# Earlier start-up work, layer norm ahead of low parts, and the first two groups' scores moved into the last projection units of an attention-plus-MLP kernel

## The chip, the cores and the metric

One core of a Trainium2 chip runs the whole layer in one launch. The metric is the time of the launch in microseconds (us), the median over runs. TensorE does matrix products and transposes (PE in the profile), VectorE elementwise work and reductions (DVE), ScalarE activations and copies (ACT), GpSimd the rest of the elementwise work (POOL); SyncE issues every DMA (SP).

## The reference

```
h  = x + softmax_attention(layernorm(x) @ wqkv) @ wo
h2 = h + silu(layernorm(h) @ w1) @ w2
```

`x` is 2048 rows by 512 in float32, `wqkv` 512 by 1536, `wo` 512 by 512, `w1` 512 by 1792 and `w2` 1792 by 512. There are 32 heads of 16 columns, the scores are scaled by 16 to the power of -0.5, and the softmax runs over all 2048 keys. The layer norm has no weights, and its epsilon is 1e-5.

## The kernel before

**Precision.** A float32 product with weights is made of three products: every operand is split into a high part and a low part (the rest), and high x high, low x high and high x low are summed in PSUM (`product`). The high part is a rounded copy; `low` subtracts it from the source on DVE. Queries and keys are split into two float16 parts, which lie beside each other in the 48 rows that the score products contract over (`sh` and `sl` in `project_qk`).

**Start.** Rows come in four blocks `b` of 512, each block in four tiles `t` of 128 rows. `load_x(0)`, then the weights of values, keys and queries (`raw_v`, `raw_qk`, 256 KB a DMA), then `load_x(1)` stand in that order in SP's queue. Block 0's layer norm is made of `statistics` (two DVE instructions and two small POOL instructions, which leave `mv` and `rs`) and `normalize` (one DVE instruction over 128x512). TensorE turns a normalized tile (four 128x128 transposes into `ps_tr`), ACT copies the high part (`xth`), DVE subtracts the low part (`xtl`). The values of block 0 are summed first over the high parts (16 products), then with the low parts (32 more). `square` and `measure` find one scale for queries and keys.

**Blocks.** For each block, two units project the first 128 columns of keys and of queries (`project_qk`, 12 products of 128x512 each), and for blocks 1 to 3 four units project the values (`project_v`). Behind a unit stand, in program order, `burst` (maxima, below), then the statistics, normalizations and turns of the next block's rows (`first_ln`, `other_ln`). In block 0 the low part of a query or key unit is on DVE; from block 1 on it is on POOL (1.17 us), in whose queue the small `rs` instructions of the next layer norm stand too. Queries and keys go to DRAM (`kd`, `qd`) and come back per head into `ks` and `qs`.

**Units.** Then come 24 units that project the rest of queries and keys (`for g in range(1, NG // 2)`).

**Maxima.** The softmax needs a bound for each row. A maximum is one score product of 128 queries by 512 keys (`ps_m`) and one DVE reduction (`mx`); there are 64 for each of the 32 items (an item is four heads and one block of queries). They are spread over the whole kernel: `BESIDE_V` says how many stand behind each unit of blocks 1 to 3, `BESIDE_A` how many stand after which product of the 24 units, and in the attention stage a planner (`maxima`) gives each group a number.

**Attention.** A group is one item and 128 keys: four score products (`ps_s`, 64 rows of the array each), four exponentials on ACT (`pt`), and, two groups later (`LAG`), four products with the values (`values`, into `pv`). The twelve `pt` tiles come from one pool. Groups 0 to 4 take four maxima each in the planner; the others take at most three. Between items 8, 16 and 24, and at the end, an MLP block runs.

**PSUM.** Eight banks are given out by pools that are opened anew for each stage: `st` (3) and `sm` (5) in the blocks, `st` (2) and `sm` (6) in the 24 units, `pv` (1), `sm` (3) and `st` (4) in the attention. A tile waits until whoever read its bank before is done. All engines run their instructions in the order in which the program issues them.

Of the kernel before, what the change touches and what calls it, by code (L numbers as in the profile page):

```python
# [20 lines left out]
P = 128  # L21
# [20 lines left out]
PTS = 12  # L42

RING = 5

# [13 lines left out]

BESIDE_V = (0, 4), (0, 4), (6, 5)  # L60

BESIDE_A = {6: 6}, {4: 4}

# [8 lines left out]
def attention_mlp_kernel(ctx: ExitStack, tc: tile.TileContext, x, wqkv, wo, w1, w2, out):  # L72
# [249 lines left out]


    with ExitStack() as pa:
# [39 lines left out]

        def measure():
# [5 lines left out]
            pool("tensor_tensor", qk_s, qk_s, expo, ALU.pow)  # L371
            dve("tensor_scalar", qk_s, qk_s, TOP / 23.0, None, op0=ALU.mult)
            dve("tensor_scalar", qk_s.bitcast(U32), qk_s.bitcast(U32), 0x7F800000, None, op0=ALU.bitwise_and)
            dve("reciprocal", qk_e, qk_s)
            dve("scalar_tensor_tensor", qk_e, qk_e, SCALE, qk_e, op0=ALU.mult, op1=ALU.mult)
            pin(nc.scalar.reg_load(qk_f, qk_e[:1, :].bitcast(U32)))

        def project_qk(b, n, beside={}, scale=False):

            g, key = divmod(n, 2)  # L380
            cols = slice(key * D + g * P, key * D + (g + 1) * P)
            ps = bank("ps_qk")
            weave(product(ps, lambda c: wqk_h[:, c, cols], lambda c: wqk_l[:, c, cols],
                          lambda c: xth[b][:, c, :], lambda c: xtl[b][:, c, :], DC),
                  {k: (lambda n=n: burst(n)) for k, n in beside.items()})
# [32 lines left out]

        found = [statistics(xts[0][:, t, :]) for t in range(4)]
        for t in range(4):  # L420
            normalize(xts[0][:, t, :], xts[0][:, t, :], *found[t])
            act("copy", wv_h[:, t, :], raw_v[:, t, :])

        def columns(t):
            return slice(t * P, (t + 1) * P)

        def turn_high(b, t):
# [11 lines left out]
        ps_vs = [bank("ps_v", "st" if t < 3 else "sm") for t in range(4)]  # L439
        for t in range(4):  # L440
            for c in range(DC):
                mm(ps_vs[t], xth[0][:, c, columns(t)], wv_h[:, c, :], start=c == 0, stop=False)
        for n in (1, 0):
            split_qk(n)
        for n in range(NG):
            square(n)
        found = {}
        for t in range(6):
            if t < 4:
                found[t] = statistics(xts[1][:, t, :])  # L450
            if 0 < t < 5:
                normalize(xts[1][:, t - 1, :], xts[1][:, t - 1, :], *found.pop(t - 1))
        for t in range(4):
            for c in range(DC):
                mm(ps_vs[t], xth[0][:, c, columns(t)], wv_l[:, c, :], start=False, stop=False)
                mm(ps_vs[t], xtl[0][:, c, columns(t)], wv_h[:, c, :], start=False, stop=c == DC - 1)
            act("copy", va[:, t, :, 0:DH], ps_vs[t].rearrange("p (h d) -> p h d", d=DH))
            if t > 0:
                ps = turn_high(1, t - 1)
                low(xtl[1][:, :, columns(t - 1)], ps, xth[1][:, :, columns(t - 1)])  # L460
            if t == 0:
                load_x(2)
        measure()

        splits = {(0, 0): 2, (0, 1): 4, (1, 1): 6, (1, 5): 3, (2, 4): 5, (2, 5): 7}

        first_ln = {0: ((), (), (3,)), 1: ((), (), ())}
        other_ln = {0: ((0, 1), (0,), ()), 1: ((2, 3), (1,), (0,)), 2: ((), (2,), (1,)), 3: ((), (3,), (2,)),
                    4: ((), (), (3,)), 5: ((), (), ())}
        for b in range(NB):  # L470
# [3 lines left out]
            for n, (kind, k) in enumerate(units + vs if b else units):  # L474
                tick()
                if kind == "v":
# [11 lines left out]
                if b + 1 < NB:  # L488
                    rows = xts[b + 1]
                    stats, norms, turns = (other_ln if b else first_ln)[n]  # L490
                    for t in stats:
                        found[t] = statistics(rows[:, t, :])
                    for t in norms:
                        normalize(rows[:, t, :], rows[:, t, :], *found.pop(t))
                    for t in turns:
                        turn_x(b + 1, t)
                if (b, n) in splits:
# [7 lines left out]

        pb.close()
        at["blocks"] = False
        open_banks(pa, 1, st=2, sm=6)
        for g in range(1, NG // 2):
            for m, (b, key) in enumerate([(b, 1) for b in range(NB)] + [(b, 0) for b in range(NB)]):  # L510
                tick()
                if g == 1 and m < 2:
                    fixed_rows(2 + m)

                n = 8 * g + m - 12
                project_qk(b, 2 * g + key, BESIDE_A[n == 19], True)
                if 0 <= n < 8:
# [6 lines left out]
    cpool = ctx.enter_context(tc.tile_pool(name="cpool", bufs=1, side="right"))  # L524
    bp = ctx.enter_context(tc.tile_pool(name="bp", bufs=PTS))
    gp = ctx.enter_context(tc.tile_pool(name="gp", bufs=2))
# [5 lines left out]
    htl = cpool.tile([P, DC, 512], F32R, name="htl")  # L532
    groups = ITEMS * KC
    pts, den = {}, {}

    def scores(g, k, kind="st"):

        i, c = divmod(g, KC)
        a, j = HEADS[k]
        assert i in placed  # L540
        ps = bank("ps_s", kind)
        mm(ps, ks[i % RING][64 * j:64 * j + 64, a, c * P:(c + 1) * P], qs[i % RING][64 * j:64 * j + 64, a, :],
           start=True, stop=True)
        pts[g, k] = bp.tile([P, 512], F32, name="pt")
        act("activation", pts[g, k], ps, AF.Exp, scale=qk_f)

    def values(g):
# [129 lines left out]
    def gate(ps, engine="dve"):  # L677
        g, gh, gl = (bp.tile([P, 512], dt, tag="pt", name=name)
                     for name, dt in (("g", F32), ("gh", F32R), ("gl", F32R)))
# [100 lines left out]
    def finish_last(pending):  # L780
# [4 lines left out]

        o_t = bp.tile([P, 4, P], F32, tag="pt", name="o_t")
        pool("memset", o_t[:, :, :64], 0.0)
# [109 lines left out]
    def maxima(g):  # L897
# [106 lines left out]
```

## Time and profile before

| what | value |
| --- | --- |
| median of 3 runs | 1692.24 us |
| lowest, highest | 1691.54 us, 1692.86 us |
| the profiled execution, its own time | 1694.05 us |
| its span, first to last instruction | 1692.3 us |
| its mean granted TensorE clock | 0.998 |
| PE, DVE, ACT, POOL busy | 98%, 86%, 73%, 16% |

The profiled execution's time is 1.75 us longer than its span: that much lies around the instructions. A row of the timeline has the start, the length, the engine, the line, the operation, the tiles as written <- read, how often it follows itself, and in brackets how long the engine had been idle and what ended that. Of a run of equal instructions the length reaches from the first start to the last end. A row of the windows has a stretch, its length, then for PE, PE's weight loads, DVE, ACT and POOL the busy time and the number of instructions, the granted clock, the share of the DMA engines that was busy, and GB/s.

### The profile page before, as it was taken

The numbers are of one execution on the slowest core, as the hardware profiler recorded it, in microseconds if no ns is written. First come the engines' busy times: TensorE is split into PE (matmuls) and PEld (weight loads), VectorE is DVE, ScalarE is ACT, GpSimd is POOL, SyncE is SP. The second block draws the span as 40 slices with busy tenths as digits, with TensorE's granted clock in tenths as the row PEclk, the third lists the DMA queues.
The fourth block names the chain that finished last, engine by engine and source line by source line (L and its number), as shares of the span: only waits on it lengthen the run. The fifth ranks groups of instructions, "written<-read, shape, count | busy, mean of one in ns | idle before, by whom it ended". The sixth has DMA issues, their size and how long they took to land.

```text
span 1692.3 us, 28327 instructions
## 1 busy us (share of the span) xinstructions
PE 1660.4 (98%) x10498; PEld 645.5 (38%) x10498; DVE 1455.0 (86%) x2428; ACT 1242.2 (73%) x2443; POOL 269.7 (16%) x441
## 2 busy tenths in 40 slices
PE   7999999999999999999999999999999999999999
PEld 6666422222245532222245532222245542222377
DVE  6899999999978889999978889999978889997343
ACT  5323599999963279999953369999963379999743
POOL 3123400000033310000033310000034310000000
PEclk9999999999999999999999999999999999999999
DMA  4434311121222111111222211111222211100222
GB/s 175 118 82 156 113 34 41 37 50 38 63 59 89 59 49 32 36 50 38 61 59 80 69 49 32 36 44 44 60 61 79 69 49 31 35 11 20 58 82 81
DMA packets 100618, 102.81 MB, mean 61 GB/s; under 512 B 19076, under 2 KB 77252, under 8 KB 100480
## 3 DMA queue, kind: packets, MB, share of 16 engines
q1 hardware_dynamic: 100480, 101.01, 20.4%
q8 instruction: 82, 1.34, 0.3%
q14 instruction: 56, 0.46, 0.1%
HBM read 77.72 MB, written 17.29 MB: 56 GB/s over the span
## 4 chain that ended last, share of the span: by engine, by line
PE 88%; ACT 7%; DVE 3%; DMA 1%; issue 1%; SPq 0%; POOL 0%; ACTq 0%; POOLq 0%
PE pv L79 34%; PE ps_s L79 19%; PE ps_m L79 11%; PE ps_acc L79 10%; ACT pt L93 6%; PE ps_qk L79 5%; PE ps_wo L79 3%; PE ps_v L79 3%; PE ps_w L79 2%; DVE mx L219 2%; PE ps_tr L82 1%; SPq L99 0%; DVE pvs L96 0%; DMA ks<-in_A_x_dram 0%; DMA ks<-kd 0%
## 5 line engine op out<-in xcount | busy, mean ns | idle before, releaser
L219 DVE TENSOR_REDUCE mx<-ps_m 128x1 f32<-128x512 f32 x2009 | 1257.4, 682 | 89.1 <-PE ps_m L79 63.1
L93 ACT ACTIVATE pt<-ps_s 128x512 f32<-128x512 f32 x2048 | 1012.8, 608 | 21.8 <-PE ps_m L79 14.9
L79 PE MATMUL ps_s<-qs,ks 64*128 64x512 f16 x2048 | 535.6, 379 | 5.5 <-ACT pt L93 2.4
L79 PE MATMUL pv<-pt,va 128*17 128x512 f32 x4096 | 538.2, 599 | 1.2
L79 PE MATMUL ps_m<-ks,qs 48*128 48x512 f16 x2009 | 506.7, 381 | 4.1 <-DVE mx L219 3.6
L79 PEld LDWEIGHTS <-ks 64*128 64x128 f16 x2048 | 148.8, 94 | 546.9 <-issue 437.6
L79 PEld LDWEIGHTS pv<-pt,va 128*17 128x17 f32 x4096 | 68.7, 95 | 227.4 <-issue 209.8
L79 PEld LDWEIGHTS <-qs 48*128 48x128 f16 x2048 | 118.4, 94 | 69.0 <-issue 64.2
L93 ACT CAST w2h<-w 128x512 fp32r<-128x512 f32 x56 | 34.8, 621 | 101.8 <-PE ps_acc L79 101.8
L93 ACT ACTIVATE g<-pv 128x512 f32<-128x512 f32 x39 | 23.3, 597 | 102.2 <-PE pv L79 102.2
L79 PE MATMUL ps_acc<-w2l,gh 128*128 128x512 f32 x224 | 92.8, 414 | 0.0
L79 PE MATMUL ps_acc<-w2h,gh 128*128 128x512 f32 x224 | 91.8, 410 | 0.0
L79 PE MATMUL ps_acc<-w2h,gl 128*128 128x512 f32 x224 | 88.0, 393 | 0.0
L86 POOL TENSOR_TENSOR w2l<-w,w2h 128x512 fp32r<-128x512 f32 x42 | 53.7, 1280 | 164.4 <-ACT w2h L93 164.4
L96 DVE TENSOR_TENSOR gl<-g,gh 128x512 fp32r<-128x512 f32 x53 | 37.0, 699 | 48.5 <-ACT gh L93 48.5
L93 ACT ACTIVATE ks<-ps_qk,qk_s 128x512 f32<-128x512 f32 x30 | 20.7, 689 | 71.7 <-PE ps_qk L79 68.8
L79 PE MATMUL pv<-htl,w1h 128*128 128x512 f32 x156 | 65.5, 420 | 0.0
L86 POOL TENSOR_SCALAR nm<-nm 128x16 f32<-128x16 f32 x51 | 12.9, 253 | 328.5 <-DVE nm L229 325.2
L86 POOL TENSOR_TENSOR mx<-mx 128x32 f32<-128x32 f32 x38 | 9.5, 250 | 345.2 <-DVE mx L219 343.6
L79 PE MATMUL pv<-hth,w1h 128*128 128x512 f32 x156 | 62.3, 399 | 0.0
L86 POOL TENSOR_TENSOR ot<-ot,den 128x512 f32<-128x512 f32 (+1 forms) x16 | 20.4, 1274 | 257.9 <-DMA den<-dr 227.1
L79 PE MATMUL pv<-hth,w1l 128*128 128x512 f32 x156 | 61.3, 393 | 0.0
(125 smaller groups left out, 1386.3 us busy)
## 6 DMA issues: line engine op xcount, KB each, us to landing
w<-in_B_w_dram SPq DMA_DIRECT2D x112, 256.0 KB
ks<-kd SPq DMA_DIRECT2D x120, 192.0 KB
qs<-qd SPq DMA_DIRECT2D x128, 48.0 KB
kd<-sh SPq DMA_DIRECT2D x16, 256.0 KB
qd<-sh SPq DMA_DIRECT2D x16, 256.0 KB
hx<-in_A_x_dram SPq DMA_DIRECT2D x16, 256.0 KB
out_dram<-ot SPq DMA_DIRECT2D x16, 256.0 KB
ot<-pvs SPq DMA_DIRECT2D x124, 32.0 KB
```

Of the source, the lines that this page charges most:

```text
L79: tc.keep_in_program_order(nc.tensor.matmul(*a, **k))
L82: tc.keep_in_program_order(nc.tensor.transpose(*a))
L86: tc.keep_in_program_order(getattr(nc.gpsimd, op)(*a, **k))
L93: pin(getattr(nc.scalar, fn)(*a, **k))
L96: pin(getattr(nc.vector, fn)(*a, **k))
L219: pin(nc.vector.tensor_reduce(mx[i][:, j, a, qt, kb:kb + 1], ps, axis=AX.X, op=ALU.max))
```

## The change

1. At the start, 24 and then 8 transposes of the identity are put ahead of and behind the first tile's transposes (`idle`). The first tile is normalized after two tiles' statistics instead of four; products with the high parts begin between the transposes; two of the four copies of the values' weights go from ACT to POOL. Squares are spread out; only two of block 1's tiles are turned ahead of `measure`, the other two behind the first key unit.
2. In units of queries and keys the next block's statistics and normalizations are issued ahead of the projection (`layer_norm`), and so ahead of its low part in POOL's queue. Turns stay behind the maxima.
3. `BESIDE_V` rises from (0, 4), (0, 4), (6, 5) to (0, 4), (2, 4), (6, 6): 72 maxima instead of 64. In the last block the first of each burst takes an `st` bank. In the first four of the 24 units, the six maxima stand after product 10, 9, 8 and 7 instead of 6.
4. The eight score products of groups 0 and 1 stand in the last two of the 24 units, each followed by a maximum: three after product 3 and three after product 9 of the last but one (with one maximum more), two after product 4 of the last (with four maxima more). They use `sm` banks. The planner gives groups 0 and 1 nothing, and the others at most three. By the end of group 4, 226 maxima are done in both kernels: 206 and 20 before, 217 and 9 after. From group 5 on, the numbers per group are the same.
5. `wv_h` and `wv_l` get a pool of their own on the right side of SBUF, and 8 of the 12 `pt` tiles take that place; the other 4 stay where `pt` was.

```diff
+EARLY = 8
-BESIDE_V = (0, 4), (0, 4), (6, 5)
-BESIDE_A = {6: 6}, {4: 4}
+BESIDE_V = (0, 4), (2, 4), (6, 6)
+BESIDE_A = {6: 6}
+BESIDE_A1 = 10, 9, 8, 7
...
+    def pt_tile(name, dtype=F32):
+        pool_of = pools[next(taken) % PTS >= EARLY]
+        return pool_of.tile([P, 512], dtype, tag="pt", name=name)
...
+        wvp = pb.enter_context(tc.tile_pool(name="wvp", bufs=1, side="right"))
-        wv_h = wp.tile([P, DC, D], F32R, name="wv_h")
-        wv_l = wp.tile([P, DC, D], F32R, name="wv_l")
+        wv_h = wvp.tile([P, DC, D], F32R, name="wv_h")
+        wv_l = wvp.tile([P, DC, D], F32R, name="wv_l")
...
+        def idle(n):
+            ps = bank("ps_i")
+            for c in range(n):
+                tr(ps[:, columns(c % 4)], ident, ident)
...
-        turned = [turn_high(0, t) for t in range(4)]
+        idle(24)
+        found = [statistics(xts[0][:, t, :]) for t in range(2)]
...
+        first_rows(0)
+        idle(8)
+        for c in range(2):
+            act("copy", wv_h[:, c, :], raw_v[:, c, :])
+        found += [statistics(xts[0][:, t, :]) for t in range(2, 4)]
+        for c in range(2, 4):
+            pool("tensor_copy", wv_h[:, c, :], raw_v[:, c, :])
+        first_rows(1)
+        first_products(0, 0)
+        first_rows(2)
+        first_products(0, 1)
+        first_rows(3)
...
-        measure()
+        turned = [turn_high(1, t) for t in range(2)]
+        measure(lambda: normalize(xts[1][:, 3, :], xts[1][:, 3, :], *found.pop(3)))
+        for t in range(2):
+            low(xtl[1][:, :, columns(t)], turned[t], xth[1][:, :, columns(t)])
...
-        first_ln = {0: ((), (), (3,)), 1: ((), (), ())}
+        first_ln = {0: ((), (), (2, 3)), 1: ((), (), ())}
...
                 else:
+                    layer_norm()
                     project_qk(b, k, scale=b > 0)
...
-                    burst(BESIDE_V[b - 1][kind == "v"])
+                    burst(BESIDE_V[b - 1][kind == "v"], *[bank("ps_m")] * (b == NB - 1))
+                if kind == "v":
+                    layer_norm()
+                for t in turns:
+                    turn_x(b + 1, t)
...
+        first_scores = [(g, m ^ (g % 2)) for g in range(LAG) for m in range(4)]
+        def begin_scores(n):
+            for _ in range(n):
+                g, k = first_scores.pop(0)
+                scores(g, k, "sm")
+                one_max(1 - HEADS[k][1])
+        BESIDE_T = {3: lambda: begin_scores(3), 9: lambda: (begin_scores(3), burst(1))}, {4: lambda: (begin_scores(2), burst(4))}
...
+        pools.append(ctx.enter_context(tc.tile_pool(name="bp0", bufs=EARLY, side="right")))
...
+                beside = {BESIDE_A1[m]: 6} if g == 1 and m < len(BESIDE_A1) else BESIDE_A
+                if n >= 18:
+                    beside = BESIDE_T[n - 18]
...
-        if g < LAG + 3:
-            at["due"] = 1
-            return 4
-        if g in marks or g - 1 in marks:
+        if g < LAG or g in marks or g - 1 in marks:
             return 0
```

More of the change, by code (lines that the diff above doesn't have):

```diff
@@ L321, in weave, with scores @@
                 inserts[k + 1]()
+    groups = ITEMS * KC
+    pts, den, pools = {}, {}, []
+    taken = iter(range(10 ** 6))
+    def pt_tile(name, dtype=F32):
+        pool_of = pools[next(taken) % PTS >= EARLY]
+        return pool_of.tile([P, 512], dtype, tag="pt", name=name)
+    def scores(g, k, kind="st"):
+        i, c = divmod(g, KC)
+        a, j = HEADS[k]
+        assert i in placed
+        ps = bank("ps_s", kind)
+        mm(ps, ks[i % RING][64 * j:64 * j + 64, a, c * P:(c + 1) * P], qs[i % RING][64 * j:64 * j + 64, a, :],
+           start=True, stop=True)
+        pts[g, k] = pt_tile("pt")
+        act("activation", pts[g, k], ps, AF.Exp, scale=qk_f)
     with ExitStack() as pa:
@@ L384, in project_qk @@
                           lambda c: xth[b][:, c, :], lambda c: xtl[b][:, c, :], DC),
-                  {k: (lambda n=n: burst(n)) for k, n in beside.items()})
+                  {k: n if callable(n) else (lambda n=n: burst(n)) for k, n in beside.items()})
             sh = xp.tile([P, 512], F16, name="sh")
@@ L417, in attention_mlp_kernel @@
         load_x(1, parts=4)
[L419 to L422, printed above, removed]
         def columns(t):
             return slice(t * P, (t + 1) * P)
+        def idle(n):
+            ps = bank("ps_i")
+            for c in range(n):
+                tr(ps[:, columns(c % 4)], ident, ident)
         def turn_high(b, t):
@@ L432, in turn_high, with first_rows, first_products @@
             return ps
-        turned = [turn_high(0, t) for t in range(4)]
+        idle(24)
+        found = [statistics(xts[0][:, t, :]) for t in range(2)]
+        turned, ps_vs = [], []
+        def first_rows(t):
+            normalize(xts[0][:, t, :], xts[0][:, t, :], *found[t])
+            turned.append(turn_high(0, t))
+        def first_products(t, *chunks):
+            if t == len(ps_vs):
+                ps_vs.append(bank("ps_v", "st" if t < 3 else "sm"))
+            for c in chunks:
+                mm(ps_vs[t], xth[0][:, c, columns(t)], wv_h[:, c, :], start=c == 0, stop=False)
+        first_rows(0)
[10 more added lines that the diff above has]
+        first_rows(3)
+        for chunks in ((0, 1), (2,), (3,)):
+            for t in range(2):
+                if t or chunks != (0, 1):
+                    first_products(t, *chunks)
+        for t in range(2, 4):
+            first_products(t, *range(DC))
         for c in range(DC):
@@ L438, in attention_mlp_kernel @@
             low(xtl[0][:, :, columns(t)], turned[t], xth[0][:, :, columns(t)])
-        ps_vs = [bank("ps_v", "st" if t < 3 else "sm") for t in range(4)]
-        for t in range(4):
[L441 to L451, printed above, removed]
+        keys = [n for n in range(NG) if n % 2]
+        split_qk(1)
+        for n in keys[:3]:
+            square(n)
+        split_qk(0)
+        found = {}
+        for t in range(4):
+            found[t] = statistics(xts[1][:, t, :])
+            if t:
                 normalize(xts[1][:, t - 1, :], xts[1][:, t - 1, :], *found.pop(t - 1))
@@ L457, in attention_mlp_kernel @@
             act("copy", va[:, t, :, 0:DH], ps_vs[t].rearrange("p (h d) -> p h d", d=DH))
-            if t > 0:
-                ps = turn_high(1, t - 1)
-                low(xtl[1][:, :, columns(t - 1)], ps, xth[1][:, :, columns(t - 1)])
             if t == 0:
                 load_x(2)
-        measure()
+                for n in (*keys[3:], *range(0, NG, 2)):
+                    square(n)
+        turned = [turn_high(1, t) for t in range(2)]
+        measure(lambda: normalize(xts[1][:, 3, :], xts[1][:, 3, :], *found.pop(3)))
+        for t in range(2):
+            low(xtl[1][:, :, columns(t)], turned[t], xth[1][:, :, columns(t)])
         splits = {(0, 0): 2, (0, 1): 4, (1, 1): 6, (1, 5): 3, (2, 4): 5, (2, 5): 7}
-        first_ln = {0: ((), (), (3,)), 1: ((), (), ())}
+        first_ln = {0: ((), (), (2, 3)), 1: ((), (), ())}
         other_ln = {0: ((0, 1), (0,), ()), 1: ((2, 3), (1,), (0,)), 2: ((), (2,), (1,)), 3: ((), (3,), (2,)),
@@ L475, in attention_mlp_kernel, with layer_norm @@
                 tick()
+                rows, (stats, norms, turns) = None, ((), (), ())
+                if b + 1 < NB:
+                    rows = xts[b + 1]
+                    stats, norms, turns = (other_ln if b else first_ln)[n]
+                def layer_norm():
+                    for t in stats:
+                        found[t] = statistics(rows[:, t, :])
+                    for t in norms:
+                        normalize(rows[:, t, :], rows[:, t, :], *found.pop(t))
                 if kind == "v":
@@ L486, in attention_mlp_kernel @@
                 if b:
-                    burst(BESIDE_V[b - 1][kind == "v"])
[L488 to L496, printed above, removed]
+                    burst(BESIDE_V[b - 1][kind == "v"], *[bank("ps_m")] * (b == NB - 1))
[3 more added lines that the diff above has]
+                    turn_x(b + 1, t)
                 if (b, n) in splits:
@@ L515, in attention_mlp_kernel @@
                 n = 8 * g + m - 12
-                project_qk(b, 2 * g + key, BESIDE_A[n == 19], True)
+                beside = {BESIDE_A1[m]: 6} if g == 1 and m < len(BESIDE_A1) else BESIDE_A
+                if n >= 18:
+                    beside = BESIDE_T[n - 18]
+                project_qk(b, 2 * g + key, beside, True)
                 if 0 <= n < 8:
@@ L524, in attention_mlp_kernel @@
     cpool = ctx.enter_context(tc.tile_pool(name="cpool", bufs=1, side="right"))
-    bp = ctx.enter_context(tc.tile_pool(name="bp", bufs=PTS))
+    bp = ctx.enter_context(tc.tile_pool(name="bp", bufs=PTS - EARLY))
+    pools.append(bp)
     gp = ctx.enter_context(tc.tile_pool(name="gp", bufs=2))
@@ L532, in attention_mlp_kernel @@
     htl = cpool.tile([P, DC, 512], F32R, name="htl")
[L533 to L545, printed above, removed]
     def values(g):
@@ L677, in gate @@
     def gate(ps, engine="dve"):
-        g, gh, gl = (bp.tile([P, 512], dt, tag="pt", name=name)
-                     for name, dt in (("g", F32), ("gh", F32R), ("gl", F32R)))
+        g, gh, gl = (pt_tile(name, dt) for name, dt in (("g", F32), ("gh", F32R), ("gl", F32R)))
         act("activation", g, ps, AF.Silu)
@@ L784, in finish_last @@
         pvs = last.pop()
-        o_t = bp.tile([P, 4, P], F32, tag="pt", name="o_t")
+        o_t = pt_tile("o_t").rearrange("p (t n) -> p t n", n=P)
         pool("memset", o_t[:, :, :64], 0.0)
```

3 lines of the change are left out of this document (2 added, 1 removed).

## The prediction

> **What bounds the kernel now.** I read the page's busy times first, then a table of windows by stage, then the timeline wherever TensorE waits in the stages that the change touches.
>
> ```profile
> PE 1660.4 (98%) x10498; PEld 645.5 (38%) x10498; DVE 1455.0 (86%) x2428; ACT 1242.2 (73%) x2443; POOL 269.7 (16%) x441
> ...
> 53.84:76.45 22.61, 21.19 (x106) 15.15 (x104) 18.50 (x35) 8.35 (x15) 5.57 (x10) 1.00 0.52 105
> 76.45:100.13 23.68, 22.98 (x106) 14.30 (x105) 19.89 (x33) 5.62 (x10) 3.29 (x3) 1.00 0.28 69
> 100.13:105.06 4.93, 3.77 (x19) 2.51 (x19) 4.40 (x8) 0.00 (x0) 0.00 (x0) 1.00 0.00 0
> 105.06:182.03 76.97, 76.97 (x371) 48.78 (x370) 75.21 (x124) 27.68 (x44) 27.40 (x38) 1.00 0.42 133
> 300.00:400.00 100.00, 99.90 (x761) 22.17 (x761) 95.76 (x160) 99.69 (x204) 4.54 (x16) 1.00 0.17 41
> ```
>
> TensorE is busy 98% of the span. In a quiet stretch of the attention (300 to 400 us) PE and ACT are both full and DVE has 4% left: 204 exponentials in 100 us make 51 groups of 1.96 us. The order and the number of maxima per group are the same from group 5 on, so nothing is to be won or lost there: what the change is worth is how much earlier group 5 begins. All of that lies before about 207 us, where PE's idle time is some ten waits of 0.1 to 1.4 us, a late start, and a slow entry into the attention.
>
> **Start.**
>
> ```profile
> 7.60 2.05 DVE L96 TENSOR_SCALAR ks<-ks,mv,rs 128x512 f32<-128x512 f32 x4
> 7.42 2.62 ACT L93 CAST wv_h<-va 128x512 fp32r<-128x512 f32 x4 [5.42 <-DMA va<-in_A_wqkv_dram]
> 8.17 3.67 PE L82 MATMUL ps_tr<-ident,ks 128*128 128x128 f32 x16 [8.17 <-DVE ks L96]
> 11.50 5.02 PE L79 MATMUL ps_v<-wv_h,xth 128*128 128x512 f32 x16
> 16.36:25.15 8.79, 8.79 (x48) 7.32 (x46) 6.41 (x14) 7.69 (x20) 3.75 (x8) 1.00 0.32 117
> 24.57 0.60 PE L82 MATMUL ps_tr<-ident,ks 128*128 128x128 f32 x4
> 28.59 2.79 PE ps_qk L79 x12
> ```
>
> TensorE begins slowly: 16 transposes take 3.67 us where 4 take 0.60 later, and 16 products take 5.02 us (0.31 each) where twelve take 2.79 (0.23). Together that is about 1.5 + 1.3 = 2.8 us. The first transposes wait for DVE, which makes four tiles' statistics before it normalizes one.
>
> After the change the first normalization comes about 1.5 us sooner; 24 idle transposes of 0.23 us (3.67/16) from about 1.5 us on (an estimate) reach to about 7 us, so the first real ones start there instead of at 8.17. I take it that they wake TensorE. Then ACT sets the pace: a copy of the first tile at about 7.7, two casts of weights (2.62/4 = 0.65 each), the copies of the other three tiles, to about 11.2; the last eight products of 0.23 follow, and the low products start at about 13.3 instead of 16.36, 3.0 us sooner. POOL's two casts (bound below by ACT's 0.65, above by POOL's 1.17 for a subtraction of that size, quoted below) end near 10.3 to 11.5; the products that need them come at 10.6 to 11.3, so the upper bound costs under 1 us. The next stage (8.79 us) loses four transposes (0.45 us) and its first key unit starts at about 21.8.
>
> Half of that gain is given back one unit later. Behind the key unit now stand two tiles' turns instead of one; with them the ring of three `st` banks comes round, and the query unit needs the bank of the key unit, which DVE reads until its low part is made:
>
> ```profile
> 29.72 0.75 DVE L96 SCALAR_TENSOR_TENSOR sl<-ps_qk,qk_s,sh 128x512 f16<-128x512 f32 x1 [1.35 <-ACT sh L93]
> 31.39 0.70 ACT sh L93
> 32.12 0.76 DVE sl L96
> 32.90 2.15 DMA qd<-sl
> 37.53 4.12 DMA ks<-kd
> 41.69 0.61 PE ps_m L79 x4
> ```
>
> The key unit ends at 24.6; 0.2 + ACT 0.70 + DVE 0.76 later, at 26.3, the query unit may start, against 28.59 - 0.25 = 28.34 before: 2.0 us sooner. The same five rows are the chain to block 1's first maximum: low part, DRAM write, the way back into `ks` (4.12 us), and PE takes it at 41.69, 0.04 us after it lands. So this maximum comes 2.0 us sooner and no more. If the transposes don't wake TensorE, the products gain nothing, and the new bank wait costs about 0.9: +0.9.
>
> **Layer norm ahead of the low part.**
>
> ```profile
> 35.53 1.17 POOL L86 TENSOR_TENSOR sl<-ks,sh 128x512 f16<-128x512 f32 x1 [7.93 <-ACT sh L93]
> 36.67 0.22 POOL L86 TENSOR_SCALAR rs<-mv 128x1 f32<-128x1 f32 x1
> 38.18 0.66 PE L82 MATMUL ps_tr<-ident,ks 128*128 128x128 f32 x4 [1.38 <-DVE ks L96]
> 61.01 0.63 PE L82 MATMUL ps_tr<-ident,ks 128*128 128x128 f32 x4 [1.42 <-ACT sh L93]
> ```
>
> POOL makes the low part before the small `rs` instructions that a normalization, and so PE's turn, waits for: 1.38 us in block 1 and 1.42 us in block 2. Both waits go. In block 1 the gain is nil: PE then reaches the maxima 1.4 us sooner, and the chain above holds it there (that wait for `ks<-kd` is what comes late next, about 1.5 us). In block 2 the data have long come, so 1.5 us are won; behind the moved POOL instructions stands the low part and its DMA, 1.6 us later, for keys that are needed a block afterwards.
>
> **More maxima in blocks 2 and 3.**
>
> ```profile
> 80.57 0.37 PE L79 MATMUL ps_m<-ks,qs 48*128 48x512 f16 x1 [0.35 <-DVE mx L219]
> 85.03 0.37 PE L79 MATMUL ps_m<-ks,qs 48*128 48x512 f16 x1 [0.35 <-DVE mx L219]
> 102.94 0.82 PE L79 MATMUL ps_m<-ks,qs 48*128 48x512 f16 x6 [1.16 <-DVE mx L219]
> 182.03 0.82 PE L79 MATMUL ps_m<-ks,qs 48*128 48x512 f16 x6
> 184.85 7.46 DVE L219 TENSOR_REDUCE mx<-ps_m 128x1 f32<-128x512 f32 x12
> ```
>
> A unit of twelve products with six maxima takes 3.74 us (76.97 us hold twenty such units and a half), twelve alone 2.79: six cost 1.0 us, and two about 0.5, since each burst also pays for its start. Block 2: two bursts of two, +1.0, against the 1.5 won: -0.5. Block 3: six units of 3.74 = 22.4 instead of 23.68, as the two waits of 0.35 go with the sixth bank: -1.2. DVE needs 7.46/12 = 0.62 per maximum, 3.7 per unit, so it just keeps up. The first of the 24 units waits 1.16 us for DVE now. Afterwards DVE has six maxima of the last burst to end, not five (+0.6), and PE comes 0.9 later: the wait shrinks, but the next three bursts follow each other one product sooner (3.5 us) than DVE can (3.7). I take -0.1 from there to the fifth unit, bounds -0.5 and +0.5.
>
> **The entry into the attention.**
>
> ```profile
> 192.12 0.69 ACT L93 ACTIVATE ks<-ps_qk,qk_s 128x512 f32<-128x512 f32 x1 [2.35 <-PE ps_qk L79]
> 192.88 0.62 ACT L93 CAST sh<-ks 128x512 f16<-128x512 f32 x1
> 193.40 4.56 ACT L93 ACTIVATE pt<-ps_s 128x512 f32<-128x512 f32 x9
> 202.07 2.07 ACT L93 ACTIVATE pt<-ps_s 128x512 f32<-128x512 f32 x4 [1.72 <-PE ps_m L79]
> 204.57 2.06 ACT L93 ACTIVATE pt<-ps_s 128x512 f32<-128x512 f32 x4 [0.42 <-PE ps_m L79]
> 207.05 17.80 ACT L93 ACTIVATE pt<-ps_s 128x512 f32<-128x512 f32 x36 [0.42 <-PE ps_m L79]
> 196.25 4.80 DVE L219 TENSOR_REDUCE mx<-ps_m 128x1 f32<-128x512 f32 x8
> 194.75:198.16 3.41, 2.66 (x11) 0.43 (x10) 3.31 (x7) 3.23 (x8) 0.03 (x1) 1.00 0.57 126
> 198.16:201.58 3.42, 3.42 (x13) 0.31 (x12) 2.89 (x5) 1.77 (x3) 0.00 (x0) 0.50 0.91 208
> ```
>
> Group 0 starts its exponentials at 193.40 and group 5 at 207.05: 13.65 us for five groups that at 1.96 would take 9.8. Four maxima a group are 2.5 us of DVE, and right behind a stretch in which PE waited for DVE, 3.4 us run at half the clock.
>
> After the change, counted from the last full burst (182.03, taken as the same point), the last two units hold 24 products (24 x 0.235), three insertions of 6, 7 and 8 small ones (0.11 each and 0.3 per start) and three waits for a bank: the first trio takes the banks of the burst before, and its last two wait for DVE (0.7); the seventh of the second trio waits for an exponential (0.4); the last unit's eight go round the ring of six (0.5). Worked through, the last product starts near 194.45 instead of 191.68: 2.8 us later. DVE ends its six maxima at 195.4, and group 2's first score waits for that. ACT's scaling and cast of the last unit come first (192.88 to 193.40 shows 0.52 from cast to exponential), so group 2's exponentials start near 196.2. Three groups of 1.96 later, at 202.1, group 5 starts: -5.0 from ACT; PE alone would give -5.4; I take -5.1. The clearing of `pv` waits for the last scaling and is done 0.3 us ahead of the first `values`. Without any bank wait it would be -6.6; with the half clock again, on PE's full schedule, 1.7 us less, -3.4.
>
> **Tiles in the place of the weights** I cost at nothing, for no row tells one place from another; cover there is none, ACT being full.
>
> ```profile
> L93 ACT ACTIVATE pt<-ps_s 128x512 f32<-128x512 f32 x2048 | 1012.8, 608 | 21.8 <-PE ps_m L79 14.9
> ```
>
> Sum: -2.0 - 0.5 - 1.2 - 0.1 - 5.1 = -8.9 us. The profiled execution took 1694.05 us (span 1692.3 and 1.75 around it) and would take 1685.15; it lies 1.8 above the median of 1692.24, from which I forecast 1683.3. About 0.2%, 3.4 us, is what a measurement of this kernel can tell from no change.
>
> **Rivals.** *Idle transposes don't wake the clock.* For it: in the trace PE turned real tiles from 8.17 for over 3 us and was still slow; it sped up only in the products. Against: they filled no whole stretch of 3.42 us, the length that the slow window at 198.16 has. The start then gives +0.9 instead of -2.0: 1686.2. The Trainium skill ("TensorE: Matmul & The Clock Gate", Part 4: PE-mode transpose) says that transposes don't count as busy time for the full clock. Its Part 1 has the clock decided in free-running windows of 3413 ns, and with that the trace agrees: 3.42 us at 0.50. By its rule for transposes this rival would be the case; no row of before decides it.
>
> *The half clock stays at the entry.* It followed a window with PE busy 2.66 of 3.41 us; PE waits at the new entry too, about 1.2 us between 194.4 and 196.4, but its value products come 3 us sooner. 8.9 - 1.7 = 7.2: 1685.0.
>
> *The insertions cost what the groups save.* If exponentials between two projection units hold up the scaling, and so the `ps_qk` banks, by 2 us in each of the two units, the entry gives -1 and the sum is -4.8: 1687.4. ACT is under 40% busy there (27.68 of 76.97), which speaks against it.
>
> *Slower: the new `pt` place.* If writing or reading the 8 moved tiles costs more than the old place, every group pays: from 8.9/2040 = 4.4 ns per exponential on (6.5 ns on each moved tile) the gain is gone, and 10 ns per exponential give +20.4 - 8.9: 1703.7. No row hints at a place that matters.
>
> **Chances.** Forecast 0.42, idle transposes in vain 0.30, half clock stays 0.14, insertions 0.07, slower place 0.04, and 0.03 for a gain swallowed in part so that it can't be told. The range takes in the first four with the bounds of the small terms (2.5 us below the forecast and 0.8 above the fourth): 1680.8 to 1688.2. Faster 0.92, same 0.04, slower 0.04.
>
> **What would show it.** Right: products of 0.23 us from the first on, low products near 13.3; a wait of about 1.5 us for `ks<-kd` at block 1's first maximum; no wait at the turns of blocks 1 and 2; group 2's exponentials about 2.8 us behind group 0's of before, less what came earlier; then 1.96 us per group at once. Wrong: products still 0.31 us apart past 12 us, more than 2 us of bank waits in the last two units, exponentials longer than 608 ns, or a 0.50 clock behind 194.

## The result: slower by 0.15%, and the profile after

The changed kernel takes 1695.11 us (median of 20 runs, 1691.77 to 1698.26), the kernel before 1692.53 us (median of 20 runs beside it, 1691.54 to 1694.23). The ratio is 1.0015, with a 95% interval from 1.0009 to 1.002. The forecast was 1683.3, the range 1680.8 to 1688.2. The profiled execution of the changed kernel took 1695.25 us, with a span of 1693.5; both are 1.2 us more than in the profiled execution of before.

By stage, most of the forecast gain is there, and then more than that is lost inside the 24 units. These rows of TensorE's timeline in the changed kernel begin the first maximum of block 1, the blocks' end, the second of the 24 units, and the six maxima of the last but two unit:

```profile
39.77 0.61 PE L83 MATMUL ps_m<-ks,qs 48*128 48x512 f16 x4 [1.10 <-DMA ks<-kd]
97.19 0.47 PE L83 MATMUL ps_qk<-xth,wqk_h 128*128 128x512 f32 x1 [0.44 <-DVE mx L223]
101.42 0.40 PE L83 MATMUL ps_qk<-xth,wqk_h 128*128 128x512 f32 x1
188.56 0.82 PE L83 MATMUL ps_m<-ks,qs 48*128 48x512 f16 x6
```

Before, these four stood at 41.69, 100.13, 105.19 and 182.03. So the changed kernel is 1.9, 2.9 and 3.8 us ahead, and 87 us further on it is 6.5 us behind: 10.3 us went inside the 24 units, where the prediction's sum had no loss. The waits of TensorE from 100 to 215 us (total us, times, longest) show what is new there:

```profile
PE ps_m L83 <- DMA ks<-kd: 4.2, 1, 4.2
PE ps_n L86 <- POOL ns L90: 1.8, 2, 0.9
PE ps_m L83 <- DVE mx L223: 0.6, 2, 0.4
```

Neither of the first two existed before. The chain of waits at the first one, and two windows (stretch, length, PE, weight loads, DVE, ACT, POOL, granted clock, DMA share, GB/s):

```profile
127.80 7.21 DMA ks<-kd
135.01 0.02 issue
135.03 8.40 DMA ks<-kd
143.43 0.14 issue
143.56 0.70 PE ps_m L83 x2
...
142.60:149.40 6.80, 5.84 (x14) 3.88 (x15) 1.29 (x2) 1.46 (x3) 0.78 (x1) 0.50 0.21 79
137.00:150.00 13.00, 8.78 (x29) 5.34 (x30) 5.51 (x9) 2.77 (x5) 4.66 (x12) 0.74 0.36 131
```

A maximum of item 2 needs the keys of a head that SP asks for at 135.03 and that land at 143.43. While TensorE waits, at 142.60, its clock falls to one half, and it stays there for 6.80 us. Wait and half clock together make 7.1 us: the eleventh of the 24 units began 1.86 us ahead of before, the thirteenth 5.24 us behind. The Trainium skill ("TensorE: Matmul & The Clock Gate", Part 1) describes decisions in windows of 3413 ns; the 6.80 us at half clock agree with two of them. The twenty runs spread over 6.5 us, against 2.7 for the kernel before, and the longest have a mean granted clock of 0.996, the shortest 0.999: so the half clock, and with it what the wait costs, differs from run to run.

The second new wait is at the transposes `ps_n` that turn an item's finished bound. POOL makes the bound in nine small instructions; the first and the last of them for the first item, and TensorE's second wait of this kind:

```profile
115.10 0.24 POOL L90 TENSOR_TENSOR mx<-mx 128x32 f32<-128x32 f32 x1 [3.00 <-DVE mx L223]
117.70 0.22 POOL L90 TENSOR_TENSOR ns<-nm,ns 128x16 f16<-128x16 f32 x1
...
186.81 0.23 PE L86 MATMUL ps_n<-ident_h,ns 128*32 128x128 f16 x1 [0.87 <-POOL ns L90]
```

The two waits cost 1.35 us (at 118) and 1.2 us (at 186.8) of progress. The rest of the 10.3 are some 0.6 us of small losses.

### The profile page after: what moved, and what is told of

Read it like the earlier page. It is cut to its first block, busy times and chain, and to the rows that moved or that the text cites. A ratio compares the mean times of both kernels' runs of the same rounds, so it can differ in the third digit from the quotient of the medians.

```text
span 1693.5 us, 28391 instructions
## 1 busy us (share of the span) xinstructions
PE 1663.7 (98%) x10530; PEld 651.0 (38%) x10530; DVE 1456.3 (86%) x2428; ACT 1240.5 (73%) x2441; POOL 271.0 (16%) x443
## 4 chain that ended last, share of the span: by engine, by line
PE 84%; ACT 8%; DVE 4%; DMA 2%; issue 1%; SPq 1%; POOL 0%; ACTq 0%; POOLq 0%; DVEq 0%
PE pv L83 33%; PE ps_s L83 19%; PE ps_m L83 10%; PE ps_acc L83 10%; ACT pt L97 7%; PE ps_qk L83 3%; DVE mx L223 3%; PE ps_wo L83 3%; PE ps_w L83 3%; PE ps_v L83 2%; DMA ks<-kd 1%; PE ps_tr L86 1%; SPq L103 1%; DVE pvs L100 0%; DMA ks<-in_A_x_dram 0%
## 5 line engine op out<-in xcount | busy, mean ns | idle before, releaser
L97 ACT ACTIVATE pt<-ps_s 128x512 f32<-128x512 f32 x2048 | 1012.7, 611 | 20.4 <-PE ps_m L83 13.3
```

Of the source, the lines that this page charges most:

```text
L97: pin(getattr(nc.scalar, fn)(*a, **k))
```

## The experiments

Theory 1 is that the eight more maxima ahead of the 24 units bring item 2 into use 8/6 = 1.33 units (5 us) sooner, before its keys have come. Rivals: SP's queue, held up by POOL's low parts, is too slow for whatever is asked of it; or the half clock comes of itself. All medians stand beside a median of the kernel before of 1692.4 to 1692.6.

**1 to 3: keys sooner, bound later, and both.**

```diff
# keys_sooner
-                if 0 <= n < 8:
-                    load_q(2 + n // 4, n % 4); load_k(2 + n // 4, n % 4)
+                if 0 <= n < 8:
+                    load_q(2 + n // 4, n % 4)
+                for y in {-1: (0, 1)}.get(n, (n + 2,) if 0 <= n < 6 else ()):
+                    load_k(2 + y // 4, y % 4)
# rows_later, in due_at
-            return WAIT
+            return WAIT + 1
```

> The changed kernel, with the keys of items 2 and 3 fetched from DRAM two projection units sooner (the first two heads right behind the last unit of keys). Theory 1, late keys: the eight added maxima make the second half of item 2's heads needed 1.33 units sooner, PE waits 4.22 us for ks<-kd at 139.4, and the half clock behind that wait costs about 2 more; both go: 6 to 7 us faster than the changed kernel (about 1688.5), about 4 faster than before. Theory 2, POOL: nine small instructions of an item's bound (2.8 us) stand ahead of the low parts on POOL and hold up the stores and with them all of SP's queue; the fetches then come hardly sooner, and the gain is under 2 us. Theory 3, the clock halves by itself at this place: the wait goes (4.2) and the half clock stays.

> The changed kernel, with the bound of an item that ends amid the projection units transposed and put into qs three ticks after its last maximum instead of two. In the changed kernel PE waits twice, 0.9 us each, for POOL's ns at that transpose, at 118 and at 186.8, since the item now ends with the last maximum of a burst. Theory 1, late keys: the first of these waits only shifts time into the wait for keys at 139.4, so 1.0 to 1.3 us faster than the changed kernel. Theory 2, POOL is what holds the queue: the transpose isn't on that path, 0 to 0.3 us faster.

> Both edits, the keys two units sooner and the bound a tick later. Theory 1: without the wait for keys both transposes' waits count, 6.5 + 2.3 = about 8.8 us faster than the changed kernel, 1686.3, that is 6 faster than before. Theory 2: under 2.5 us faster than the changed kernel.

Measured: 1698.07, 1691.74 and 1696.40 us. The first and the third miss theory 1's numbers by far; fetching the keys sooner made the kernel slower, which no theory had. In the first, TensorE waits for queries instead (6.8 us; in the third 8.9), and SP's timeline shows why:

```profile
123.29 0.84 SPq L103 DMA_DIRECT2D qd<-sl  x1
131.27 0.71 SPq L103 DMA_DIRECT2D qs<-qd  x1
...
140.10 1.11 PE L83 MATMUL ps_m<-ks,qs 48*128 48x512 f16 x4 [4.88 <-DMA qs<-qd]
148.66 0.54 PE L83 MATMUL ps_m<-ks,qs 48*128 48x512 f16 x2 [1.95 <-DMA qs<-qd]
```

SP issues nothing from 124.1 to 131.27: its next instruction fetches queries that the stores just ahead of it write, these stand behind two fetches of keys, and the second store takes 7.9 us to land. Everything behind that fetch waits too. So SP's queue is held up, as theory 2 had it, but by a store, not by POOL. The later bound took both `ps_n` waits away, as expected, and won 3.4 us by the medians (2.2 by the spans), not 1.0 to 1.3: in its profile one window of half clock follows the wait for keys (4.5 us there), not two.

**4: 64 maxima again.** Edit: `BESIDE_V = (0, 4), (0, 4), (6, 5)` in the changed kernel.

> The changed kernel, with the maxima beside blocks 2 and 3 as they were before, (0, 4) and (6, 5): 64 instead of 72 ahead of the 24 units. Theory 1: item 2 is needed 1.33 units later, the wait of 4.22 us and the half clock go (6 to 7 us), the transposes' waits fall elsewhere, blocks 2 and 3 give 1.0 + 0.35 us back in addition, and the eight maxima have to be done in the first attention groups (DVE 0.62 us each, at 3 a group no more than 0.5 us a group lost, up to 2 us): 1686 to 1689. Theory 2: the bound's instructions move by 5 us and collide with other low parts, so about as slow as the changed kernel, 1693 to 1696.

Measured: 1710.00 us, far outside both. Yet its first 400 us are what theory 1 said: no wait for keys, and group 5's exponentials begin at 197.1, 10.0 us ahead of before (forecast -8.9 with all 72). Then 27 us are lost in the attention, which begins with eight maxima fewer done, and the items' bounds come too late. Its waits of TensorE from 400 us on, and the two longest of its five stretches of half clock (23.8 us in all):

```profile
PE ps_s L83 <- DMA qs<-mt: 9.5, 4, 2.9
PE ps_n L86 <- POOL ns L90: 6.3, 2, 3.1
...
611.00:617.80 6.80, 6.42 (x27) 1.28 (x31) 3.96 (x7) 3.97 (x8) 0.24 (x2) 0.50 0.13 43
1003.50:1010.30 6.80, 5.33 (x23) 1.12 (x23) 2.88 (x6) 2.87 (x6) 1.09 (x5) 0.50 0.28 94
```

So the eight maxima can't be left out either: with the new entry, which does fewer of them, they are what keeps the later bounds in time.

**5: all of item 2 sooner** (with the later bound): `load_k` of heads 0 and 1 behind the last unit of keys, two heads' `load_q` and one `load_k` behind each of the next two units.

> The changed kernel with the bound a tick later (as in the second experiment), and all eight fetches of item 2, its queries as well as its keys, behind the last unit of keys and the first two units of queries: the last two heads come two units sooner than in the changed kernel; item 3's stay where they were. Theory 1, as amended by the first experiment (item 2's heads are needed sooner than keys and queries land): in the second experiment the only wait left was 4.5 us, with one half-clock window behind it (1.7); both go, 1691.7 - 6 = 1685.7, between 1684.5 and 1687. Theory 2 (SP's queue, held up by the low parts, can't bring all this sooner): another fetch is late by 2 to 6 us, 1690 to 1696.

Measured: 1693.76 us; theory 2's number. SP stands still from 123.7 to 130.6 as in the first experiment, the last keys are asked for at 135.51 after all, and TensorE goes on at 144.18, 8.7 us later. (The profile names a store that landed at 144.09 as what released it; that the keys landed then is inferred.)

**6: the 72 maxima alone, in the kernel before.** Edit: `BESIDE_V = (0, 4), (2, 4), (6, 6)` there.

> The kernel before, with the number of maxima beside the blocks of the change alone: (0, 4), (2, 4), (6, 6) instead of (0, 4), (0, 4), (6, 5). Theory 1: this alone makes item 2 needed too soon; a wait of 3 to 5 us for ks<-kd in the eleventh of the 24 units, up to two half-clock windows (3.4) behind it, and 1.0 + 0.4 + 1 in the blocks: 5 to 9 us slower than before, 1697 to 1701. Rival: the wait comes of the earlier start of the units against the DMA queue (layer norm and start), not of the maxima; then no wait here, and 1 to 2.5 us slower than before.

Measured: 1704.84 us, 12.3 slower than before and so beyond the 5 to 9 expected, with a wait in the eleventh of the 24 units that has the same chain, and two half-clock windows:

```profile
131.75 7.63 DMA ks<-kd
139.38 0.02 issue
139.39 8.45 DMA ks<-kd
147.84 0.14 issue
147.98 0.71 PE ps_m L79 x2
...
147.30:154.10 6.80, 6.12 (x15) 3.95 (x15) 1.29 (x2) 1.46 (x3) 1.06 (x1) 0.50 0.22 84
```

It began its second unit 1.1 us behind before, not ahead, and waits all the same: the maxima do it, not the earlier start. The two `ps_n` waits are there as well (1.8 us in its table of waits). These two transposes, 1.2 us each, were not in the expectation, nor 0.9 us that the entry takes longer; with 1.1 up to the second unit and some 7 for the wait and its half clock that makes 11.4 of the 11.6 us by which group 5 starts later (218.67 against 207.05).

**7: no idle transposes** (on the fifth kernel): both calls of `idle` taken out.

> The kernel of the fifth experiment without the 32 transposes of the identity at the start. The prediction's forecast: they wake TensorE's clock; without them the first products are 0.31 us apart or more, the low products start near 16 instead of 13.3, and the first maximum of block 1 about 2.9 us later: 2.9 slower than the fifth experiment. Rival (transposes do nothing for the clock): the first products are as fast as with them, within 0.3 us.

Measured: 1696.18 us, 2.4 slower than the fifth; block 1's first maximum comes 2.7 us later (42.24 against 39.52). TensorE's start with them (the changed kernel, four rows, of the idle ones the first twenty) and without (the last four):

```profile
1.48 4.53 PE L86 MATMUL ps_i<-ident 128*128 128x128 f32 x20 [1.48 <-POOL ident masks.py:199]
6.38 0.60 PE L86 MATMUL ps_tr<-ident,ks 128*128 128x128 f32 x4
10.57 3.51 PE L83 MATMUL ps_v<-wv_h,xth 128*128 128x512 f32 x14
13.91 0.39 PE L83 MATMUL ps_v<-wv_l,xth 128*128 128x512 f32 x1
...
5.96 1.11 PE L86 MATMUL ps_tr<-ident,ks 128*128 128x128 f32 x4 [5.96 <-DVE ks L100]
11.17 1.05 PE L86 MATMUL ps_tr<-ident,ks 128*128 128x128 f32 x4
11.88 4.55 PE L83 MATMUL ps_v<-wv_h,xth 128*128 128x512 f32 x14
16.27 0.40 PE L83 MATMUL ps_v<-wv_l,xth 128*128 128x512 f32 x1
```

Four transposes take 0.60 us at 6.38 with them and 1.05 us at 11.17 without. The twenty take 0.22 us each ((4.53 - 0.42)/19, with 0.42 for the last), the next real ones half of that. The transposes did bring the full speed, alone.

**8: the old entry** (on the fifth kernel): no scores in the last two units, `{4: 4}` in the last, four maxima in each of groups 0 to 4.

> The kernel of the fifth experiment with the entry into the attention as before: no scores in the last two projection units, six maxima and then four beside them, four per group in groups 0 to 4 (so 234 instead of 226 are done by group 5). The prediction's term for the entry is -5.1 us; counted from the six maxima of the last but two unit, group 5's exponentials then start 5.1 us later than in the fifth experiment (25.0 instead of 19.95 us behind that burst), less up to 1.7 if no half-clock window falls there. Rival (the insertions cost what the groups save): 0 to 2 us later.

Measured: 1699.62 us. The six maxima of the last but two unit and group 5's exponentials, old entry and then the fifth kernel's new one:

```profile
187.94 0.82 PE L83 MATMUL ps_m<-ks,qs 48*128 48x512 f16 x6
213.10 3.10 ACT L97 ACTIVATE pt<-ps_s 128x512 f32<-128x512 f32 x6 [0.42 <-PE ps_m L83]
...
187.82 0.82 PE L83 MATMUL ps_m<-ks,qs 48*128 48x512 f16 x6
202.01 14.30 ACT L97 ACTIVATE pt<-ps_s 128x512 f32<-128x512 f32 x29
```

25.2 us with the old one. With the new one the twelve exponentials of groups 2 to 4 (0.48 to 0.49 each) stand between 202.01 and group 5, which starts at 207.78: 20.0. The entry is worth 5.2 us at group 5, though the old one does eight maxima more by then.

**9 and 10: item 2's first two heads first.** Its 64 maxima went through both pairs of heads for each block of keys; now the pair is the outer loop. No fetch moves.

```diff
+    for j in range(2):
+        todo[2, j].sort(key=lambda work: work[3])
# the tenth also: return WAIT + 1
```

> The changed kernel with item 2's maxima in another order and nothing else: all 32 of its first two heads ahead of the 32 of the other two, so that the last two heads' fetches are needed 24 maxima, four units or 15 us, later. The fetches and the queue of SP stay as they are. Theory 1 (the fetches of the last two heads of item 2 are needed too soon): the wait of 4.22 us at 139.4 goes, and with it the two half-clock windows (142.6 to 149.4, 6.8 us, of which up to 3.4 are lost): 1695.1 - 4.2 - 2 to 3.4 = 1687.5 to 1689. Theory 2 (the queue of SP as a whole is too slow, whatever is asked for): the first two heads or item 3 are late instead, gain under 2 us.

> As the ninth, and the bound of an item transposed a tick later (as in the second experiment). Theory 1: both transposes' waits, 1.35 and 1.2 us, now count in full: 2.5 faster than the ninth, 1685 to 1686.5, that is 6 to 7.5 faster than before and near the forecast less 0.3 of small losses. Theory 2: as slow as the second experiment, 1691 to 1692.

Measured: 1687.92 us (ratio to before 0.9976, 0.9967 to 0.9985) and 1685.49 us (0.9965, 0.9951 to 0.9979): theory 1's numbers both times. The two intervals overlap; by the spans the tenth is 2.2 us faster than the ninth. In the ninth the stretch around the old wait is full, at full clock. The two longest entries of its waits from 30 to 260 us are the two `ps_n`, which the tenth hasn't got, and the keys of block 1 and of item 2's first heads:

```profile
137.00:150.00 13.00, 13.00 (x63) 8.35 (x62) 11.66 (x20) 4.39 (x8) 5.93 (x13) 1.00 0.42 150
PE ps_n L86 <- POOL ns L90: 1.8, 2, 1.0
PE ps_m L83 <- DMA ks<-kd: 1.7, 2, 1.2
```

The same fetches, in the same queue, are in time once their keys are needed later, and the half clock goes with the wait, so it didn't come of itself. What the change broke was the deadline. The tenth is the fastest version here by its median, and faster than both kernels.

**11: layer norm behind the low part again** (on the tenth): `layer_norm()` after `burst` in units of queries and keys.

> As the tenth, with the layer norm of the next block behind the low part again in units of keys and queries. The prediction's term: nothing in block 1 (the maxima wait for keys there anyway), 1.4 to 1.5 us lost in block 2. So the wait of about 1.4 us at block 2's first turn comes back, the 24 units begin 1.5 us later, and the kernel is 1.5 us slower than the tenth. Rival (block 1's wait counts too): 2.9 slower; rival (something else waits at that place anyway): 0 to 0.4.

Measured: 1686.69 us, 1.2 slower than the tenth by the medians, though the two intervals overlap. By stage it is 1.3: the first of the 24 units starts at 97.77 against 96.46. In the trace of the eleventh the wait of 1.36 us is back in block 1, and in block 2 only 0.53 us of waiting, not the 1.4 expected:

```profile
36.32 0.66 PE L86 MATMUL ps_tr<-ident,ks 128*128 128x128 f32 x4 [1.36 <-DVE ks L100]
59.20 0.63 PE L86 MATMUL ps_tr<-ident,ks 128*128 128x128 f32 x4 [0.53 <-ACT ks L97]
```

Behind block 1's first maximum the loss is 0.6 us: from there to the first of the 24 units the eleventh takes 58.00 us, the tenth 57.44. The other 0.75 stands ahead of that maximum (39.77 in the eleventh, 39.02 in the tenth), and there one profile each can't decide: with the layer norm ahead, that maximum comes at 39.02 to 39.99 from run to run.

**12: queries first** (on the tenth): all four `load_q` and one `load_k` behind the first unit of queries, two `load_k` behind the second, one behind the third.

> The tenth kernel, with item 2's fetches in an order in which no fetch stands in SP's queue behind a store that it has to wait for and that itself waits behind big fetches: all four heads' queries and one head's keys behind the first unit of queries, two heads' keys behind the second, one behind the third. In the fifth experiment SP issued nothing from 123.8 to 130.6, its next instruction being a fetch of queries that needs a store issued behind two fetches of keys. If that order was what undid the earlier fetches there, SP now stands still under 3 us at this place, the last fetch of item 2 is issued near 131 instead of 135.2, the two waits of 0.9 and 0.6 us left at the first maxima of item 2 go, and the kernel takes 1684 to 1685.5. If SP's queue can't take more in this stretch whatever the order, the last fetch is issued past 134 and the kernel takes 1685.5 to 1688.

Measured: 1689.42 us, outside both expectations and slower than the tenth by the medians, though the two intervals overlap. The standstill of SP is gone, as expected, and the last keys are asked for at 132.71, between the two numbers, but the second head's keys now stand 1.6 us later in the queue, and that is what TensorE meets first:

```profile
126.88 8.77 DMA ks<-kd
135.65 0.14 issue
135.78 0.73 PE ps_m L83 x4
```

The wait there is 2.2 us, against 0.9 at the same place in the tenth. In the chains of waits that were read, a fetch of a head's keys took 6.3 to 8.8 us from issue to landing, and there was no room to spend 1.6 us. Whether some order of the fetches meets the earlier deadline of the changed kernel stays open; those of experiments 1, 3 and 5 didn't.

## Why the prediction was wrong, step by step

The step that failed is the costing of "More maxima in blocks 2 and 3" and of the first units behind them ("I take -0.1 from there to the fifth unit"). It priced the eight maxima by what TensorE and DVE spend on them, and took the maxima behind them as the same work a little sooner. It never asked which item the maxima of each unit belong to, and when that item's keys land: a wait for keys in the 24 units was put at nothing, without a reason. With 64 ahead, item 2 begins after the fourth maximum of the eleventh unit and needs its last two heads in the thirteenth; with 72 it begins in the tenth and needs them in the eleventh. The fetches stayed behind the same units, and the last one took 8.4 us to land. The prediction checked just this for block 1's first maximum ("the chain above holds it there"), and not for item 2. It cost 4.2 us and the half clock behind it, 7.1 together; no rival had it. The sixth experiment shows that the maxima alone bring the wait, the fourth that it goes without them, the ninth that it goes as well when the last two heads are needed later. The chain was there to be priced from the trace of before: the fetch of item 2's last head, and the first burst in the thirteenth unit that needs it:

```profile
138.41 0.71 SPq L99 DMA_DIRECT2D ks<-kd  x1
148.46 0.82 PE L79 MATMUL ps_m<-ks,qs 48*128 48x512 f16 x6
```

That is 10.05 us from issue to use. With 8.4 us for the fetch (the changed kernel's; before shows no landing here) some 1.6 us were to spare, an estimate, and the eight maxima asked for 5 us.

A second, smaller miss has the same root: shifted by eight, two items end with the last maximum of a burst, so POOL's nine small instructions on the bound no longer fit in front of the transpose two ticks (projection units) later: 2.5 us by stage.

The other steps, measured by stage:

| step | forecast | measured |
| --- | --- | --- |
| start, to block 1's first maximum | -2.0 | -1.9 |
| layer norm and two bursts, to block 3 | -0.5 | -0.3 (76.45 to 74.28) |
| block 3 | -1.2 | -0.8 (100.13 to 97.19) |
| the 24 units, to the start of the fifth | -0.1 | -0.4 (116.40 to 113.05) |
| the other units, to the burst of the last but two | 0 | +9.9 |
| entry, from there to group 5 | -5.1 | -5.1 (25.0 to 19.96) |
| attention from group 5 to the end | 0 | -0.3 |

- Block 3 and the units behind it: together -1.2 against -1.3. The wait for DVE in the first unit fell from 1.16 to 0.36 us, and the next three bursts gave back half of that, as the prediction said in words.
- Start: right in mechanism, in size partly by luck. Low products and key unit both came 0.6 us later than worked out (13.91 and 22.39), and the wait for an `st` bank before the query unit is there (0.69 us, released by DVE's `sl`). So the query unit began at 26.98, 1.4 us sooner than before and not 2.0. That block 1's first maximum still came 1.9 sooner is within what the way of the keys into `ks` differs by: in the ten profiles with this start and the layer norm ahead it comes at 39.02 to 39.99.
- The clock at the start: right, and the rival "idle transposes don't wake the clock" (0.30) is refuted: in the seventh experiment the products are slow again without them. The rule of the Trainium skill that it rested on ("TensorE: Matmul & The Clock Gate", Part 4: PE-mode transpose) doesn't hold here; the measurement decides.
- Layer norm: the two waits are gone, as forecast. Its worth of 1.5 us in block 2 isn't what the eleventh experiment shows: 0.6 there, and between nothing and 0.75 in block 1, which the prediction had at nothing. In the eleventh two maxima stand ahead of the turn in block 2 (at 58.28) that the kernel before hasn't got, and they may fill part of the wait; that was not varied by itself. The chain for `ks<-kd`, whose end moves by 1 us from run to run, held less firmly than the prediction took it to.
- The entry: right to 0.1 us, in part by luck. Group 2's exponentials begin 14.2 us behind the burst at 188.56, as worked out (196.2 less 182.03), and run on without a gap:

```profile
202.74 9.89 ACT L97 ACTIVATE pt<-ps_s 128x512 f32<-128x512 f32 x20
L97 ACT ACTIVATE pt<-ps_s 128x512 f32<-128x512 f32 x2048 | 1012.7, 611 | 20.4 <-PE ps_m L83 13.3
```

  The bank waits were smaller than worked out, 0.23, 0.25 and 0.28 us, 0.8 us less in all; yet the last product starts 12.5 us behind the burst, as worked out (194.45 less 182.03), so the rest of that sum was as much too small. ACT, not TensorE, set the end, as forecast. No half clock fell there, and the entry gave what was forecast, so the rivals "half clock stays" and "insertions cost what they save" fall.
- The new place of the tiles: the second row above has 611 ns for an exponential against 608, and 1012.7 us in all against 1012.8. It costs nothing that can be told.
- The chances: the four faster cases add up to 0.93, where the prediction has 0.92.

Put together, the tenth kernel, which is the change without its two stumbling blocks, lies at 1685.49: 2.2 above the forecast and inside its range. It is another kernel than the one that was predicted, so this bears out the other terms and not the forecast.

## What to carry to other kernels

Work that is moved ahead takes its inputs' deadlines with it: list, for every consumer that comes sooner, who fetches its data, when that is issued and how long it takes to land, and subtract. When data come too late, look first whether other work of the same kind can be done in the meantime; here two lines that reordered the maxima won 7 us, where four attempts at moving fetches in SP's queue each gave a kernel that was slower, by the medians, than without the move. Price a wait of TensorE with the half clock that can follow it: here 4.2 us became 7.

## What the runs showed of the hardware

- Transposes alone brought TensorE to full speed. The first twenty idle transposes stand 0.22 us apart; from about 6.2 us on, with nothing but transposes ahead of them, they stand 0.11 apart (four in 0.60 us, of which the last takes 0.27). The column of the granted clock reads 1.00 throughout this start, so the spacing has to be read instead.
- SP's issue looks limited by transfers under way. In the changed kernel the keys' fetch issued at 135.03 is the eighth after that of 127.80, and it was issued 0.02 us after that one had landed; in the sixth experiment the same holds for 139.39 and 131.75. That was not varied by itself.
- A wait of TensorE of 4.2 us was followed by two windows of 3.4 us at half the clock in the changed kernel, one of 4.5 us by a single one in the second experiment.
